# A decay factor's way to the partitions: one transfer of 128 pieces of 16 bytes, and a re-sorted instruction order, in a fused gated linear attention and MLP mixer

## The chip, the cores and the metric

The kernel runs on one core of a Trainium2 chip. The core has TensorE (PE in the profile; its weight loads are PEld), VectorE (DVE), ScalarE (ACT), GpSimd (POOL) and SyncE (SP), each with an instruction queue of its own, worked off in order. 16 DMA engines serve the transfers that SP and POOL issue here. The metric is the time of one execution on the device in microseconds (us). The kernel before takes 181.18 us in the median of three runs (180.58, 181.18 and 183.98).

## The reference

Inputs are q, k, v and f_logit of shape (4, 8, 768, 48): batch, heads, positions, head width. First comes a linear attention whose state decays by a gate per key channel, then an MLP mixer over tokens and channels.

```python
f = 1.0 / (1.0 + np.exp(-f_logit))
for t in range(S):
    state = f[:, :, t, :, None] * state + np.einsum('bhd,bhe->bhde', k[:, :, t], v[:, :, t])
    y[:, :, t] = np.einsum('bhd,bhde->bhe', q[:, :, t], state)
x = y.transpose(0, 2, 1, 3).reshape(B, S, H * D)          # (4, 768, 384)
h = np.maximum(x.transpose(0, 2, 1) @ w_tok1, 0.0) @ w_tok2   # 768 -> 256 -> 768
u = x + h.transpose(0, 2, 1)
out = u + np.maximum(u @ w_ch1, 0.0) @ w_ch2              # 384 -> 1536 -> 384
```

## The kernel before

The 768 positions of a batch are cut into six chunks of 128. Within a chunk the recurrence is turned into matrix products. With S(t) the running sum of -log f from the chunk's start, the queries are scaled by exp(-S), the keys by exp(S), and the state is carried from chunk to chunk with the factor exp(-S(127)), one number per head and key channel.

The steps of one chunk, with the names and lines that the change and the prediction touch:

- `gates` (L473, L474, L479): ACT makes exp(-f) and L = log(1 + exp(-f)); DVE or POOL makes `Llo`, the part of L that its upper 16 bits lose. L is read as two bf16 halves. In batch 2 the planner chooses DVE or POOL for Llo, in batch 3 it is POOL.
- sums (L535 to L547): PE multiplies by a triangle of ones and leaves the running sums in a PSUM bank. For the first two batches it makes, in the same bank, the sums of the whole chunk with the key channels on the partitions (eight products with a column of ones).
- `G`, `Gi` (L559, L557): ACT makes exp(-S) and exp(S), and DVE scales q and k (L579).
- transposes (L589), copies of them (`qkT`, L455, L602), scores (L496), the mask product (`AmT`, DVE, L626), the products of keys and values (L512).
- the factor of the chunk, `glast[4]`, tiles of 128 partitions by 4 floats: partition = 64 x (head modulo 2) + key channel, column = head pair. In the first two batches it is an exponential of the column sums (L562). In the last two, ACT makes the exponential of the last 32 rows of the running sums in the natural layout into `ends` (L566), whose row 127 is the wanted one, and SP spreads that row over the partitions by DMA (L570 to L573), one transfer for each head pair.
- the state update on DVE (`tsum` L638, `state` L635 and L640, which read `glast`), two copies of it to bf16 (`state_bd`, L453 on ACT, L457 on POOL), and the chunk's output (L657 with the old state, L664 within the chunk), copied out as `x_bf` and `x_nat` (L453, L455).

From batch 1 on two chunks go together. When a batch's six chunks are there, `mixer` runs: tok1 (L694, relu into `h1T`, L462, L464), tok2 (L710) with the sums `x_nat` and `u_bf` (L726), transposes `ut` (L745), the first channel product "C1" (L762, 24 groups of three matmuls of 384 columns, relu into `zT`) and the second "C2" (L781, with the last sum on DVE, L787, and a store by SP, L791). The mixer of one batch runs mixed with the attention of the next.

All instructions are first written into a list of operations (`Plan`), with what each needs and makes, a rank (a due time) and a listed cost. `order` goes through them like a list scheduler: for each engine's ready operations it takes the one that could start first, counting a listed `lag`, then by rank. `SHIFTS` gives hundreds of operations, by their number, a rank and a lag of their own; such a table is the outcome of a search over orders. The resulting order is the program order, queue by queue; nothing is decided at run time, and the semaphores are put in for that order. Filler matmuls (L828) are put where the planner sees PE wait in the first 25 us. The bulk loads stand in POOL's queue among its computing (L394, L401), in a fixed order with computing sorted between them.

The operation of the transfer carries a listed cost: `("fix", 1900, 7000 if b == 2 else 4500, 520)`, that is 1900 ns of SP's time, 7000 or 4500 ns until the factor is there, and 520 ns of the wire.

Of the kernel before, what the change touches and what calls it, by code (L numbers as in the profile page):

```python
# [10 lines left out]
FP32 = mybir.dt.float32  # L11
# [9 lines left out]
    (24,60,100), (34,-50,2100), (40,-50,3100), (41,-50,1700), (50,50,1600), (73,-30,800), (76,0,600),  # L21
    (79,30,300), (80,60,700), (82,60,500), (84,90,1400), (98,300,800), (101,300,3200), (103,300,2200),
    (109,-106,0), (115,0,400), (116,0,600), (123,0,800), (124,0,800), (125,0,1200), (126,0,1100), (129,30,700),
    (130,30,300), (134,30,900), (138,30,1500), (141,30,900), (142,30,1000), (144,30,900), (146,30,1600),
    (148,30,2900), (149,30,3400), (150,60,1800), (154,60,600), (156,60,1600), (157,60,800), (163,60,2100),
    (164,60,2400), (165,60,1600), (167,60,1800), (168,60,1700), (169,60,1200), (170,60,600), (172,90,800),
    (173,90,1900), (176,90,1100), (177,90,500), (178,90,2500), (181,90,1500), (182,90,2000), (185,90,1900),
    (188,90,2700), (191,90,2900), (193,90,3100), (196,120,1100), (198,120,1200), (199,120,1500),
    (200,120,1500), (201,120,1700), (202,120,2200), (204,120,700), (215,120,3700), (216,150,500),
    (217,150,1000), (219,150,1100), (220,150,700), (221,150,1400), (222,150,900), (223,150,2100),  # L30
    (224,150,2400), (225,150,1900), (227,150,2800), (229,150,2500), (230,270,1800), (231,270,2300),
    (238,191,2300), (239,275,3600), (244,275,1500), (246,280,1000), (251,281,600), (253,301,3100),
    (257,302,2700), (258,283,1600), (262,284,1700), (265,284,3000), (269,285,300), (270,290,1200),
    (271,290,1500), (272,291,1300), (274,292,1300), (276,293,1200), (278,294,1200), (279,294,2300),
    (280,295,1000), (281,295,1500), (282,-89,0), (283,300,2000), (284,623,0), (286,310,200), (287,310,300),
    (288,-160,0), (289,315,2400), (290,-161,0), (292,53,0), (293,325,2200), (294,252,0), (296,335,100),
    (297,335,100), (298,-125,0), (299,340,2000), (300,446,0), (302,302,0), (303,350,1200), (304,947,100),
    (306,462,0), (307,360,600), (309,365,500), (310,164,0), (311,370,1200), (312,-610,200), (313,375,600),
    (314,914,0), (316,586,0), (318,157,0), (319,390,800), (320,395,300), (321,395,200), (322,-236,0),
    (323,400,1800), (324,312,0), (325,405,900), (326,410,100), (327,410,500), (328,415,100), (330,547,0),  # L40
    (332,770,0), (333,420,800), (335,690,0), (338,460,600), (341,513,100), (342,527,400), (345,1125,0),
    (347,567,300), (350,580,400), (355,620,200), (357,854,400), (363,318,0), (367,438,500), (370,449,0),
    (371,595,0), (373,490,700), (384,383,0), (385,370,300), (391,429,0), (400,360,2200), (401,360,700),
    (406,360,1000), (408,360,1400), (411,360,1100), (415,360,1000), (416,360,1800), (419,440,2200),
    (422,581,0), (423,440,500), (428,440,1300), (430,440,500), (439,440,1800), (440,440,1100), (442,440,2200),
    (444,440,600), (445,440,700), (446,440,900), (447,440,800), (451,440,400), (452,440,800), (457,520,800),
    (459,520,400), (465,520,200), (477,520,100), (478,520,300), (479,520,100), (480,413,0), (483,520,100),
    (486,580,400), (487,720,400), (490,580,300), (492,581,400), (494,821,400), (504,563,0), (508,583,600),
    (516,580,100), (518,581,500), (520,582,500), (523,583,900), (525,584,900), (526,797,0), (527,585,900),
    (528,420,0), (531,697,600), (532,302,0), (534,645,0), (535,711,900), (536,809,0), (538,307,0), (542,837,0),  # L50
    (543,739,900), (544,860,0), (546,852,0), (548,829,0), (550,812,0), (552,427,0), (555,781,100), (556,873,0),
    (560,771,0), (561,802,500), (562,846,0), (564,670,0), (565,816,400), (566,915,0), (567,823,300),
    (568,1027,0), (570,652,0), (572,754,0), (573,844,1700), (574,745,0), (576,909,0), (578,1039,0),
    (579,860,300), (581,966,0), (587,965,200), (588,980,100), (591,995,100), (592,1010,600), (593,1025,300),
    (594,995,600), (596,1381,0), (597,855,0), (610,590,300), (616,690,300), (618,790,400), (621,790,400),
    (622,790,600), (623,790,1000), (625,620,100), (627,869,0), (630,620,500), (631,620,1100), (633,754,0),
    (634,815,0), (638,620,600), (639,620,1500), (645,620,1800), (646,620,1300), (648,620,2600), (651,620,200),
    (652,620,1600), (653,620,1600), (654,620,1500), (660,620,700), (661,720,400), (662,720,1100),
    (663,720,1200), (664,720,1000), (666,720,1400), (668,720,600), (669,363,500), (670,720,700), (671,720,200),
    (672,720,800), (677,880,0), (682,720,800), (684,720,1000), (689,720,1100), (690,789,0), (691,720,900),  # L60
    (693,720,800), (697,720,500), (698,720,100), (699,869,0), (701,820,1100), (705,920,0), (706,820,300),
    (720,820,700), (721,820,600), (723,906,0), (724,820,1600), (725,820,1600), (745,780,0), (748,823,0),
    (751,919,0), (753,972,1900), (756,973,1700), (757,969,0), (760,975,300), (761,975,600), (762,975,1400),
    (769,1130,0), (770,973,800), (777,1399,300), (778,1087,900), (785,1166,0), (786,1115,1200), (787,1072,0),
    (789,1269,0), (791,1206,0), (793,1193,0), (795,1043,0), (797,1109,0), (798,1157,900), (803,1178,300),
    (804,1178,1100), (805,1105,300), (806,1185,800), (807,1192,200), (809,1090,0), (811,1206,700),
    (812,1206,1900), (813,1213,400), (814,1213,2000), (815,1220,600), (816,1220,2200), (817,1227,800),
    (818,1227,1500), (821,1241,900), (822,1241,1700), (824,1265,300), (828,1295,3800), (830,1325,5400),
    (833,1340,1300), (834,1355,3200), (838,1385,1500), (840,1415,4500), (841,1385,5400), (845,1460,3700),
    (848,1475,1800), (849,1490,4600), (854,980,1200), (856,980,1600), (860,1080,3000), (863,1080,1900),  # L70
    (865,1180,1300), (870,1180,1400), (872,1010,2500), (885,1010,200), (891,1010,1000), (892,1010,400),
    (894,1010,700), (895,1010,700), (898,1010,1700), (899,1010,900), (900,1010,1600), (902,1010,800),
    (907,1010,1100), (908,1039,0), (911,1110,800), (913,959,1000), (915,1110,1900), (916,1099,0),
    (918,1110,800), (919,1110,600), (921,1110,600), (922,1175,0), (923,1110,800), (928,1110,700),
    (929,1110,1200), (933,1110,4200), (934,1438,0), (938,1110,1000), (939,1110,1200), (944,1110,2500),
    (945,1110,2200), (946,1210,300), (947,1210,1000), (948,1210,1200), (949,1210,800), (951,1210,800),
    (957,1210,1900), (970,1210,1300), (971,1210,2300), (973,1210,3200), (976,1210,2100), (977,1210,3200),
    (978,1360,1000), (985,1361,900), (992,1360,1400), (994,1360,5900), (995,1361,2200), (998,1362,3100),
    (1000,1362,4500), (1001,1363,2000), (1004,1364,2900), (1005,1364,3300), (1006,1364,8300), (1007,1365,3800),
    (1008,1365,5000), (1011,1360,5100), (1017,1363,6600), (1019,1364,4700), (1021,1365,7000), (1022,1470,3000),  # L80
    (1023,1470,7300), (1025,1477,4600), (1027,1484,3900), (1028,1491,5200), (1030,1498,3900), (1032,1505,5300),
    (1035,1512,3700), (1036,1519,5900), (1037,1519,5900), (1038,1526,5700), (1040,1533,4600), (1044,1547,5300),
    (1047,1554,6700), (1048,1561,4800), (1052,1575,5100), (1056,1423,0), (1060,1603,5600), (1062,1610,4900),
    (1063,1610,6000), (1065,1617,4600), (1066,1624,5900), (1068,1631,5800), (1075,1685,5400), (1085,1775,5700),
    (1090,1820,5600), (1092,1850,4700), (1095,1865,4800), (1096,1880,5100), (1102,1929,4900),
)
KEPT = 3
# [212 lines left out]
def kernel(  # L300
# [12 lines left out]
    nc = tc.nc  # L313
# [208 lines left out]
    def sums_and_turns(b, c, r):  # L522
# [42 lines left out]
        elif not last:  # L565
# [4 lines left out]
            def across():  # L570
                row = ends[i][127:128].rearrange("o (hp par) d -> o hp (par d)", par=2)
                for hp in range(HP):
                    nc.sync.dma_start(out=glast[g4][:, hp:hp + 1], in_=row[:, hp])  # L573
# [288 lines left out]
```

## Time and profile before

| what | value |
|---|---|
| median of three runs | 181.18 us |
| the profiled execution | 180.21 us |
| its span | 178.5 us |
| PE busy | 168.8 us (95%) |
| DVE, ACT, POOL busy | 130.7, 117.7, 84.9 us |
| clock granted to PE | 1.0 throughout |
| factor transfers (L573) | 40, of 0.5 KB each |
| packets of SP's and POOL's DMA queues | 15600 and 78960 |

The profile is taken of one execution; its own time lies 1.71 us above its span. An engine's busy time says how full it is, not what ends a stretch. On PE each matmul's record overlaps the next, so the distance between starts tells what one costs. In a list of waits, each line gives the waiting group, what ended its wait, the time in total, how often, and the longest.

### The profile page before, as it was taken

The page shows a single profiled execution, that of the slowest core. Times are in us where ns is not written, and L with a number is a line of the kernel's source. Part 1 is how long each engine was busy: PE and PEld are TensorE (multiplying, and loading weights), DVE is VectorE, ACT ScalarE, POOL GpSimd, SP SyncE. Part 2 cuts the span into 40 slices and gives each one's busy share as a digit, 9 for nine tenths or more (in the row PEclk, how much of TensorE's full clock was granted, in tenths as well). Part 3 has the DMA queues.
Part 4 walks back from the last instruction along what each step waited for, and adds up shares of the span by engine and source line. Part 5 has one row for each costly group of instructions (what it writes and reads, how often), then busy time and mean ns, then how long its engine had stood idle before and what let it go on. Part 6 is the DMA issues. An engine that isn't in the chain of part 4 may idle for free.

```text
span 178.5 us, 4470 instructions
## 1 busy us (share of the span) xinstructions
PE 168.8 (95%) x1739; PEld 108.0 (61%) x1739; DVE 130.7 (73%) x284; ACT 117.7 (66%) x272; POOL 84.9 (48%) x111
## 2 busy tenths in 40 slices
PE   6989977999999998999999999999999999999992
PEld 2446545566767765666667565766676666667660
DVE  6789876968987999995969777988967375423231
ACT  4589794869984398989899847488864333376000
POOL 7999968639299659589444750330111011000000
PEclk9999999999999999999999999999999999999999
DMA  7999999999999999999999990110001002210132
GB/s 106 122 163 160 142 207 217 242 147 194 165 141 174 220 167 189 52 109 91 231 131 118 190 141 19 45 47 1 6 2 44 4 2 93 82 48 0 44 132 88
DMA packets 94581, 19.97 MB, mean 112 GB/s; under 512 B 87296, under 2 KB 93744, under 8 KB 94560
## 3 DMA queue, kind: packets, MB, share of 16 engines
q0 software_dynamic: 78960, 13.77, 96.4%
q1 hardware_dynamic: 15600, 5.92, 13.8%
q8 instruction: 13, 0.21, 0.5%
q14 instruction: 8, 0.07, 0.1%
HBM read 25.17 MB, written 4.72 MB: 167 GB/s over the span
## 4 chain that ended last, share of the span: by engine, by line
PE 66%; DVE 9%; ACT 7%; issue 6%; DMA 4%; POOL 4%; SPq 1%; DVEq 0%; ACTq 0%; POOLq 0%
PE ps L781 20%; PE ps L762 20%; PE ps L589 4%; PE ps L710 4%; DMA f_sb<-in_f_logit_dram 3%; PE ps L496 2%; PE ps L828 2%; PE ps L694 2%; POOL qk_sb L394 2%; DVE AmT L626 2%; PE ps L745 2%; PE ps L664 2%; PE ps L512 1%; DMA glast<-ends 1%; PE ps L547 1%
## 5 line engine op out<-in xcount | busy, mean ns | idle before, releaser
L781 PE MATMUL ps<-w_ch,zT 128*128 128x384 bf16 (+2 forms) x300 | 52.7, 320 | 0.0
L762 PE MATMUL ps<-uT,w_ch 128*128 128x384 bf16 x288 | 51.3, 326 | 0.0
L462 ACT ACTIVATE zT<-ps 128x384 bf16<-128x384 f32 x71 | 34.2, 490 | 14.5 <-PE ps L762 12.1
L781 PEld LDWEIGHTS <-zT 128*128 128x128 bf16 x300 | 27.6, 98 | 16.5 <-issue 0.5
L762 PEld LDWEIGHTS <-w_ch 128*128 128x128 bf16 x288 | 27.0, 98 | 16.5
L626 DVE TENSOR_TENSOR AmT<-ps,tri_bf 128x512 bf16<-128x512 f32 x46 | 30.3, 683 | 5.5 <-PE ps L496 5.5
L787 DVE TENSOR_TENSOR x_nat<-x_nat,ps 128x384 f32<-128x384 f32 (+2 forms) x25 | 13.3, 533 | 14.1 <-PE ps L781 12.0
L394 POOL DMA_DIRECT2D qk_sb<-in_q_dram x19 | 18.5, 974 | 9.1 <-DMA w_ch<-in_moe_w_ch_dram 3.4
L394 POOL DMA_DIRECT2D qk_sb<-in_k_dram x19 | 18.9, 993 | 5.4 <-DMA f_sb<-in_f_logit_dram 4.3
L394 POOL DMA_DIRECT2D v_sb<-in_v_dram x19 | 18.7, 982 | 2.7 <-ACT L L474 2.4
L464 DVE TENSOR_SCALAR zT<-ps 128x384 bf16<-128x384 f32 x25 | 13.4, 554 | 7.2 <-PE ps L762 6.6
L579 DVE TENSOR_TENSOR qk<-qk_sb,GG 128x768 bf16<-128x768 bf16 (+1 forms) x30 | 14.3, 481 | 3.2 <-ACT GG L559 2.3
L589 PE MATMUL ps<-ident,qk 128*128 128x128 bf16 x192 | 15.0, 219 | 1.4 <-DVE qk L579 1.4
L457 POOL CAST state_bd<-state 48x192 bf16<-48x192 f32 x16 | 5.6, 352 | 21.8 <-DVE state L640 12.7
L589 PEld LDWEIGHTS <-qk 128*128 128x128 bf16 x192 | 11.9, 97 | 4.6 <-DVE qk L579 3.1
L828 PE MATMUL ps<-steady 128*128 128x512 bf16 x39 | 12.8, 438 | 1.5 <-DVE steady L426 1.5
L473 ACT ACTIVATE f_sb<-f_sb 128x384 f32<-128x384 f32 x24 | 11.9, 519 | 3.6 <-DMA f_sb<-in_f_logit_dram 3.4
L557 ACT ACTIVATE GG<-ps 128x384 bf16<-128x384 f32 x24 | 11.6, 488 | 1.8 <-PE ps L547 1.7
L726 DVE TENSOR_TENSOR x_nat<-x_nat,ps 128x384 f32<-128x384 f32 x21 | 10.9, 548 | 2.5 <-PE ps L710 2.5
L474 ACT ACTIVATE L<-f_sb 128x384 f32<-128x384 f32 x24 | 12.1, 522 | 0.3
L602 DVE COPY qkT<-ps 128x1024 bf16<-128x1024 bf16 x18 | 12.0, 683 | 0.4 <-PE ps L589 0.2
L559 ACT ACTIVATE GG<-ps 128x384 bf16<-128x384 f32 x24 | 11.6, 488 | 0.9 <-PE ps L547 0.5
(71 smaller groups left out, 244.2 us busy)
## 6 DMA issues: line engine op xcount, KB each, us to landing
out_dram<-x_nat SPq DMA_DIRECT2D x23, 192.0 KB, 1.9
f_sb<-in_f_logit_dram POOLq DMA_DIRECT2D x3, 1152.0 KB, 10.4
qk_sb<-in_k_dram POOLq DMA_DIRECT2D x18, 96.0 KB, 6.4
qk_sb<-in_q_dram POOLq DMA_DIRECT2D x18, 96.0 KB, 6.2
v_sb<-in_v_dram POOLq DMA_DIRECT2D x18, 96.0 KB, 6.4
f_sb<-in_f_logit_dram SPq DMA_DIRECT2D x6, 192.0 KB, 4.6
w_ch<-in_moe_w_ch_dram POOLq DMA_DIRECT2D x2, 576.0 KB, 10.2
w_ch<-in_moe_w_ch_dram POOLq DMA_DIRECT2D x1, 1152.0 KB, 14.6
```

The costliest lines, as they stand in the source:

```text
L394: lambda eng=eng, into=into, of=of: eng.dma_start(out=into, in_=of),
L462: nc.scalar.activation(out_, in_, AF.Relu, bias=0.0, scale=1.0)
L464: nc.vector.tensor_scalar(out_, in_, 0.0, None, ALU.max)
L474: add(ACT, r, lambda: nc.scalar.activation(full, fb, AF.Ln, bias=1.0, scale=1.0), need=[key], make=[whole], kind=el)
L579: add(DVE, r, lambda n=n: nc.vector.tensor_tensor(qk[i][:, n, :, 0:D], qk_sb[nb][:, n, :, c, :], GG[i][:, n], ALU.mult), need=[(x, nb, c) ...
L589: nc.tensor.transpose(to[:, o + hp, :], blk(src)[:, hp, :], ident)
L602: add(DVE, r, lambda: nc.vector.tensor_copy(qkT[i], banks[p_t[0].at].bitcast(BF16).rearrange("p (n t) -> p n t", t=C)), make=[("qkT", i, 0 ...
L626: add(DVE, r, lambda half=half, made=made: nc.vector.tensor_tensor(half, made(), tb4, ALU.mult), need=["tri_bf"], make=[("AmT", i, p)], ba ...
L762: nc.tensor.matmul(banks[pm.at][:, 0:384], lhsT=w[:, kt, c0:c0 + 128], rhs=uT[:, kt, cols], start=(kt == 0), stop=(kt == 2))
L781: nc.tensor.matmul(banks[pm.at][:, 0:n1 - n0], lhsT=zT[:, kt, tt * 128:(tt + 1) * 128], rhs=w_ch2[:, kt, n0:n1], start=(kt == 0), stop=(kt ...
L787: add(DVE, rank("ch2", tt), lambda un=un, pm=pm, n=n1 - n0: nc.vector.tensor_tensor(un, un, banks[pm.at][:, 0:n], ALU.add), make=[("x_nat" ...
L828: nc.tensor.matmul(banks[NBANK - 1], lhsT=steady[:, 0:128], rhs=steady, start=True, stop=True)
```

## The change

Four things change together:

1. `ends` is laid out as 128 x (2, 64, 4): parity of the head, channel, head pair, in place of 128 x (8 heads, 64 channels). The four factors of one partition lie side by side in 16 bytes.
2. The exponential that fills it writes through a permuted view: neighbouring channels lie 16 bytes apart.
3. One transfer of 128 pieces of 16 bytes takes the place of four transfers of 128 pieces of 4 bytes.
4. The listed cost of the operation becomes 600 ns, 5200 or 3400 ns, and 300 ns, and `SHIFTS` is another table. So the order of all queues differs. The operations themselves are the same, but for some that may go to either of two engines, and 38 filler matmuls for 39.

```diff
-    ends = [st([128, H, 64], FP32, f"ends{i}") for i in range(2)]
+    ends = [st([128, 2, 64, HP], FP32, f"ends{i}") for i in range(2)]
...
             add(ACT, r, lambda: nc.scalar.activation(
-                ends[i][96:128, :, 0:D], sview()[96:128], AF.Exp, bias=0.0, scale=-1.0),
+                ends[i][96:128, :, 0:D].rearrange("t par d hp -> t hp par d"),
+                sview()[96:128].rearrange("t (hp par) d -> t hp par d", par=2), AF.Exp, bias=0.0, scale=-1.0),
                 make=[("ends", i)], bank=p_s, kind=el)

             def across():
-                row = ends[i][127:128].rearrange("o (hp par) d -> o hp (par d)", par=2)
-                for hp in range(HP):
-                    nc.sync.dma_start(out=glast[g4][:, hp:hp + 1], in_=row[:, hp])
+                nc.sync.dma_start(out=glast[g4], in_=ends[i][127:128].rearrange("o par d hp -> o (par d) hp"))

             add(SP, r, across, need=[("ends", i)], make=[("glast", g4)],
-                kind=("fix", 1900, 7000 if b == 2 else 4500, 520))
+                kind=("fix", 600, 5200 if b == 2 else 3400, 300))
...
 SHIFTS = (
-    (24,60,100), (34,-50,2100), (40,-50,3100), (41,-50,1700), (50,50,1600), (73,-30,800), (76,0,600),
+    (6,-30,200), (24,60,1500), (26,60,1800), (40,-50,3400), (42,-50,2300), (44,-50,2000), (46,-50,3600),
...
```

In the changed order, as far as the prediction uses it: in batch 1 the state update of chunk 4 stands on DVE ahead of the last mask product of the pair; the sums of batch 2's chunk 1 come ahead of the last output of batch 1, so that ACT has G, Gi and `ends` of one chunk ahead of `h1T`; Llo of batch 2's chunk 2 is POOL's, behind ten loads, another Llo and the load of f for batch 3; then come the state copies of chunks 0 and 1 and the load of k; two Llo of batch 3 stand on POOL between the loads of q and v. The last stretch of PE is as before: C1 and then 84 matmuls of C2.

## Prediction

> **What bounds the kernel now.** I read four views in this order: the page's busy times, the waits of each engine, the chain of the last microseconds, and the order in time around the places where TensorE stood still.
>
> ```profile
> PE 168.8 (95%) x1739; PEld 108.0 (61%) x1739; DVE 130.7 (73%) x284; ACT 117.7 (66%) x272; POOL 84.9 (48%) x111
> PEclk9999999999999999999999999999999999999999
> ```
>
> PE is the bound, at full clock. Its busy time covers overlapping matmuls, so the chain says better how dense it is:
>
> ```profile
> 155.06 8.29 PE ps L762 x51
> 163.35 11.74 PE ps L781 x84
> ```
>
> 51 matmuls of 384 columns in 8.29 us are 162.5 ns each, and the last 20 us hold nothing else. So time can only come out of PE's standstills. The waits of PE, over the whole span:
>
> ```profile
> PE ps L589 <- DVE qk L579: 1.4, 3, 0.8
> PE ps L657 <- ACT state_bd L453: 1.1, 2, 0.6
> PE ps L710 <- DVE h1T L464: 0.5, 1, 0.5
> PE ps L710 <- ACT h1T L462: 0.4, 2, 0.3
> PE ps L745 <- DVE u_bf L726: 0.3, 1, 0.3
> PE ps L547 <- POOL Llo L479: 0.2, 1, 0.2
> ```
>
> The named waits count idle time alone. Between matmul starts the losses are larger by the pipeline's depth (0.54 idle at 69.19 is 0.70 between starts). Counted that way from 34 us on, where the first mixer begins, I find 0.70 at 69.2, 0.43 at 72.5, 0.38 at 99.3, 0.33 at 109.7, 0.31 at 140.1 and 0.27 at 57.0: 2.4 us in all. Ahead of 34 us some 5 us more are lost beside the 39 filler matmuls. None of these waits names a factor DMA, and neither does any wait of DVE, the engine that reads what it brings (L635, L640). Last, the line of the source that issues it:
>
> ```profile
> L573 SPq DMA_DIRECT2D glast<-ends x40: 469/594/1467, 70.2 to 131.5; - x40
> ...
> DMA to landing us min/median/max: 1.9/2.8/7.8
> ```
>
> The reader is to see the issue's cost on SP (ns, least, median, most) and the latency, long only where other transfers run.
>
> **The transfer itself.** Ten chunks (five in each of the last two batches) lose three of four issues: 30 issues of 0.594 us (median of L573), 17.8 us of SP's time. SP is idle most of the span, and behind these issues stand only stores of finished rows, for which nobody waits: worth 0. Latency: issues start 0.60 to 0.64 us apart, so the fourth lands about 3 x 0.6 + 2.0 = 3.8 to 3.9 us after the first issue where the queues are quiet (landing 1.9 to 2.1 after 108 us), and 6.0 to 8.7 us where the last batch's bulk loads run (82 to 107 us, landing up to 7.8). One transfer: 1.9 to 2.1 quiet, 4 to 7.8 loaded. No row shows 16-byte pieces. Bounds: not under 1.9, the least landing of the 4-byte ones; not over 2.9 quiet, what the 192 KB stores of that stretch take. I take 2.0, because the piece count of one transfer stays 128. Gain by itself: 0, since the factors lie ready 2.7 us and more before the state update that reads them. If that cover were gone (a chunk's sums put closer than 5 us of PE work to its use), lateness would cost its own length.
>
> **The exponential that feeds it (L566 before).** Ten of 0.483 us. It now writes floats 16 bytes apart. Rows of ACT with 384 elements lie between 0.47 and 0.52 whatever they write (L474, which writes 48 of each 64 floats, 0.522). No row has such a spacing, so bounds: 0 to a doubling, +0.48 each. I take 0, with the rows nearest to it, and keep 1.0 us for the range, because only two or so of the ten stand ahead of something PE waits for (the h1T at 71.97 stands behind two of them). The Trainium skill, page "SBUF — State Buffer", section "Door 1: The DMA port swizzle", speaks against this edit: accesses need two hits in a 16-byte line to run at full rate, and here each float is alone in its line. No run here shows it yet; by it the ten would be slower, by up to my upper end as an estimate.
>
> **The new order.** This is where the time can move: every queue is re-sorted. PE does the same matmuls but 38 fillers for 39 (-0.22, though a filler only stands in a wait). PE runs its list in order, so I laid both lists out and summed the issue intervals of what stands between a producer and its consumer: 0.49 for three 384-column matmuls, 0.45 for eight transposes, 0.55 for sixteen scores. What follows compares these covers with what the link needs.
>
> - Standstill at 69.2 (0.70): chunk 5 of batch 1 waits for the state copies of chunk 4. Cover after the value products is 3.46 us in both. DVE in order of time shows the update behind a mask product, which it does not need:
>
> ```profile
> 66.58 0.34 DVE L638 TENSOR_TENSOR tsum<-state,ps 128x192 f32<-128x192 f32 x1
> 66.84 0.68 DVE L626 TENSOR_TENSOR AmT<-ps,tri_bf 128x512 bf16<-128x512 f32 x1
> 67.44 0.92 DVE L640 TENSOR_TENSOR state<-tsum,glast 128x192 f32<-128x192 f32 x1
> ```
>
>   Now the update stands ahead of that product (0.60), so the copies can start 0.6 earlier; then the last mask product is late, behind an addition of 0.47, but it still ends before the old 69.1. Gain 0.5 to 0.7, taken 0.6.
> - 72.5 (0.43): the h1T of ACT stood behind three gate and two `ends` exponentials that wait on sums issued just before. Now one sum of batch 2 stands behind, and ACT has G, Gi, ends, then h1T; cover 0.98 in both, need about 0.75 (0.48 and the pipeline). Gain 0.4.
> - 99.3 (0.38): Llo of batch 3 stood behind the load of v on POOL, which waited for room. Now two Llo stand ahead of that load, and the first of these sums comes 3.2 us of PE work later. Gain 0.4.
> - 57.0 (0.27): cover from transposes to scores 1.30 for 1.18. Gain 0.1. 109.7 and 140.1: covers 1.10 for 0.98, and 0.97 for 0.97. Gain 0.
> - Head: the last x_bf on DVE no longer stands behind an x_nat copy (28.11, 0.47), so the last tok1 group is bound by ACT's x_bf (ends 28.86) and not by DVE's (29.13): 0.26. ACT's u_bf copies lose one x_nat between them (0.39), and the first C1 begins ahead of the last transposes. Together 0.5. Chunks 0 and 1 are read out later, with 3 to 4 us of cover: 0.
> - New tight places: transposes to scores of chunk 5 in batch 1, cover 0.49 and 0.28 of the other chunk's scores, need 0.95 (qkT copy 0.68): 0.2 lost. Chunks 0 and 1 there, 0.97 for two copies: 0.1. Reading out chunk 0 of batch 3, cover 1.77 for two mask products (1.36 and the pipeline), and chunk 3, 2.44 for mask, sum, update and two POOL copies: 0.2 together.
> - Llo of chunk 2 in batch 2 was on DVE and is now on POOL, behind eight loads (0.90 each), another Llo (0.83), two more loads and the 2.26 load of f. The Llo ahead of all these end near 67.5 (69.05 before, with one L fewer ahead of them on ACT): 67.5 + 7.2 + 0.8 + 1.8 + 2.3 + 0.8 = 80.4. Its L stands on ACT behind five relus, which can make it 82.4. PE comes to the sum after 69.8 us of listed work; before, the clock ran 11.1 ahead of the listed work at 69.2 and 11.8 at 82.2, so about 81.3. Loss 0 to 1.1; taken 0.4.
>
> Gains 0.6 + 0.4 + 0.4 + 0.1 + 0.5 = 2.0; losses 0.2 + 0.1 + 0.2 + 0.4 = 0.9. Net 1.1 from the profiled execution's 180.21 (span 178.5 and 1.71 around it): **179.1**. That execution is 0.97 under the median shown (181.18) and 0.37 under the fastest run (180.58), so a median of the changed kernel may lie up to 1 above what I name. About 2% is what a measurement of this kernel can tell from no change: 3.6 us, more than all standstills after 34 us together.
>
> **Rivals.** (1) The new order trades standstills one for one: 180.2, within 2%. For it: two covers are unchanged, and the order was laid out with listed costs, not with these rows. (2) Slower: POOL's line between 67 and 83 us. It carries Llo of chunk 2, then four state copies, then the 2.27 load of k. If a load there waits for room as one did before,
>
> ```profile
> 83.40 2.27 POOL L394 DMA_DIRECT2D qk_sb<-in_k_dram x1
> ...
> 91.53 2.22 POOL L394 DMA_DIRECT2D qk_sb<-in_q_dram x1 [3.40 <-issue]
> ```
>
> the Llo ends at 80.4 + 3.4 = 83.8 and PE stands 2.5 us at 81.3, in place of the 0.4 taken: 179.1 + 2.1 = 181.2. The state copies behind it (0.36 each, done at 84.5 for the first chunk) are read 1.3 us after that sum and add nothing. It decides against the change once that Llo ends after 82.8 (81.3 + 0.4 + the net 1.1); two such waits in the line make it 184.6, over 2%. Against it: what waited at 91.5 was a 576 KB load behind two large ones; those ahead of this Llo are 96 KB each but for f. (3) The strided exponential doubles: 0.48 ahead of four links, two covered: 179.1 + 1.0 = 180.1. The skill's line rule above is this rival's. (4) The transfer does not do what it says, pieces of 16 bytes costing as four did: 3.9 instead of 2.0. The tightest new link, chunk 2 of batch 3 (sum to its use 7.4 us of PE work, need 1.0 + 2.0 + 1.8), would still hold: 179.1.
>
> **Chances.** Forecast (177.8 to 179.9) 0.43, rival 1 0.2, rival 2 0.24 (half of it with a second wait or like misses elsewhere, beyond 2%), rival 3 0.1, rival 4 0.03. The range takes in rival 2 with its one wait (181.2), the median's offset (1.0) and half of rival 3 (0.5), and below it the losses of the new tight places at nothing and the head's gain at double (179.1 - 0.9 - 0.5): 177.6 to 182.7. Faster by over 2% needs 176.6, nearly all standstills gone: 0.05. Slower by over 2%: 0.12. Within: 0.83.
>
> **What would show it.** One issue per chunk landing in about 2.0 after 108 us; `ends` at 0.48; no wait of PE for state copies near 68, for h1T near 71, for Llo near 102; PE's last row still about 20 us of C1 and C2. Wrong: a wait of PE for Llo near 82, long gaps before POOL's loads there, `ends` near 0.8 or above, or a first C1 later than 34.2.

## The result, and the profile after

The changed kernel takes 182.08 us in the median of 13 runs (181.21 to 183.26), the kernel before 181.12 us in 13 runs beside them. The ratio is 1.0075 with a 95% interval of 1.0049 to 1.0101: slower by 1.4 us (0.0075 x 181.12), where the forecast was faster by 1.1. The profiled execution of after took 182.05 us, its span is 180.3. That is 1.84 over the profiled execution of before (180.21, 178.5). The two medians lie 0.96 us apart; the ratio, which comes with an interval, is what the text goes by. Ratios below are against the kernel before, each run beside its own runs of it. A few executions ran at a lower granted clock (one of e2 took 219.22 us at 0.755, and the profiled one of e3 285.77 us at 0.564), and the ratios are taken without such executions.

First the page of after, busy times and clock:

```profile
PE 169.5 (94%) x1734; PEld 108.5 (60%) x1738; DVE 131.0 (73%) x282; ACT 121.0 (67%) x275; POOL 84.5 (47%) x110
...
PEclk9999999999999999999999999999999999999998
```

PE and its clock are as before. ACT has 3.3 us more. Where they sit is seen in the lines of the exponential and of the transfer (least, median and most ns, then the first and last start), and under them the latency of the transfer:

```profile
L564 ACT ACTIVATE ends<-ps x10: 852/863/873, 69.0 to 127.2; 32x384 f32<-32x384 f32 x10
L570 SPq DMA_DIRECT2D glast<-ends x10: 469/475/560, 69.9 to 128.1; - x10
...
DMA to landing us min/median/max: 1.9/2.6/4.1
```

The transfer does what was forecast: one issue in place of four, landing in 1.93 to 1.95 where the queues are quiet (one 2.4), 2.7 to 4.1 beside bulk loads. The exponential does not: 0.863 us in place of 0.483, so 3.8 us for the ten. Next the waits of PE over the whole span (those of the filler matmuls, 1.5 and 0.2 us, are left out; the forecast's list leaves out its 1.5 too, and two waits of 0.2):

```profile
PE ps L586 <- DVE qk L576: 1.6, 4, 0.5
...
PE ps L543 <- DVE Llo L477: 0.7, 2, 0.4
PE ps L691 <- DVE x_bf L453: 0.6, 2, 0.4
PE ps L707 <- DVE h1T L462: 0.5, 1, 0.5
PE ps L494 <- DVE qkT L453: 0.4, 1, 0.4
PE ps L742 <- ACT u_bf L451: 0.2, 1, 0.2
```

The waits that the forecast took away are gone: none for the state copies (1.1 before), none for ACT's h1T, none for POOL's Llo. Others stand in their place after 34 us: for `x_bf`, for `qk`, for `u_bf`. The waits for DVE's `Llo` (0.7) and for `qkT` (0.4) lie ahead of 34 us. The end of the chain is still dense, 48 matmuls in 7.80 us and 84 in 11.74, followed by the last sum:

```profile
156.60 7.80 PE ps L759 x48
164.40 11.74 PE ps L778 x84
176.16 0.56 DVE x_nat L784
```

The last sum begins 1.04 us later than before (176.16 for 175.12). The span ends 1.8 later, so another 0.8 is lost behind the last matmul. The wait of SP's queue for that store in after:

```profile
SPq L854 <- DMA out_dram<-x_nat: 1.4, 1, 1.4
```

It names 1.4 us, but the store lands 1.82 us after its issue, as before (1.83). What follows the landing is in the records of SP's last instructions, taken from the trace of the two kernels (the time in us at which the wait is over, and the semaphore waited for, by number):

```text
before: 71 transfers of SP, the last on 117    after: 41 transfers, the last on 108
175.70  issue of the last store                176.75  issue of the last store
176.15  108                                    178.58  108 (store landed 178.57)
176.21  110                                    178.65  110
...                                            178.72  112
176.46  116                                    179.16  114
177.55  117 (store landed 177.53)              ...
177.61  118                                    179.44  118
177.67  drain                                  179.51  drain
178.49  end                                    180.34  end
```

SP's transfers take eight semaphores in turn, and at the end of the program SP waits for all eight in a fixed order. With 71 transfers the last store is on the next to last of them, and the six ahead of it are over while the store is under way. With 41 it is on the first, and the seven others follow the landing, with one step of 0.44 among them (what it waits for the trace does not name): 0.96 from landing to end before, 1.77 after, 0.8 us.

### The profile page after: what moved, and what is told of

Read it like the earlier page. It is cut to its first block, busy times and chain, and to the rows that moved or that the text cites. A ratio compares the mean times of both kernels' runs of the same rounds, so it can differ in the third digit from the quotient of the medians.

```text
span 180.3 us, 4391 instructions
## 1 busy us (share of the span) xinstructions
PE 169.5 (94%) x1734; PEld 108.5 (60%) x1738; DVE 131.0 (73%) x282; ACT 121.0 (67%) x275; POOL 84.5 (47%) x110
## 4 chain that ended last, share of the span: by engine, by line
PE 52%; DMA 17%; ACT 9%; POOL 9%; DVE 6%; issue 4%; POOLq 0%; DVEq 0%
PE ps L759 19%; PE ps L778 17%; DMA w_ch<-in_moe_w_ch_dram 8%; DMA f_sb<-in_f_logit_dram 6%; POOL qk_sb L392 5%; PE ps L586 3%; POOL v_sb L392 3%; DMA qk_sb<-in_k_dram 2%; PE ps L707 2%; PE ps L494 2%; PE ps L691 2%; DVE qk L576 2%; PE ps L742 2%; ACT ends L564 1%; ACT f_sb L471 1%
## 5 line engine op out<-in xcount | busy, mean ns | idle before, releaser
L759 PE MATMUL ps<-uT,w_ch 128*128 128x384 bf16 x288 | 52.6, 326 | 0.1
L460 ACT ACTIVATE zT<-ps 128x384 bf16<-128x384 f32 x74 | 35.6, 490 | 17.2 <-PE ps L759 12.2
L462 DVE TENSOR_SCALAR zT<-ps 128x384 bf16<-128x384 f32 x22 | 12.0, 554 | 9.0 <-PE ps L759 8.0
L576 DVE TENSOR_TENSOR qk<-qk_sb,GG 128x768 bf16<-128x768 bf16 (+1 forms) x30 | 16.1, 547 | 2.6 <-ACT GG L557 1.7
L825 PE MATMUL ps<-steady 128*128 128x512 bf16 x34 | 10.9, 430 | 1.8 <-DVE steady L424 1.5
```

What stands on the lines that cost most here:

```text
L460: nc.scalar.activation(out_, in_, AF.Relu, bias=0.0, scale=1.0)
L462: nc.vector.tensor_scalar(out_, in_, 0.0, None, ALU.max)
L576: add(DVE, r, lambda n=n: nc.vector.tensor_tensor(qk[i][:, n, :, 0:D], qk_sb[nb][:, n, :, c, :], GG[i][:, n], ALU.mult), need=[(x, nb, c) ...
L759: nc.tensor.matmul(banks[pm.at][:, 0:384], lhsT=w[:, kt, c0:c0 + 128], rhs=uT[:, kt, cols], start=(kt == 0), stop=(kt == 2))
```

## The experiments

Two explanations were set against each other at first. **Theory A**: the slower exponential, in front of what PE waits for, and the later end cost more than the new order brings. **Theory B**: the new order itself is worse. The edits are given against the kernel that each starts from.

### e1 to e4: the order, and the way the exponential writes

Old transfer in the new order (e1), and the new transfer in the old order (e2):

```diff
 e1, against after
-    ends = [st([128, 2, 64, HP], FP32, f"ends{i}") for i in range(2)]
+    ends = [st([128, H, 64], FP32, f"ends{i}") for i in range(2)]
-                ends[i][96:128, :, 0:D].rearrange("t par d hp -> t hp par d"),
-                sview()[96:128].rearrange("t (hp par) d -> t hp par d", par=2), AF.Exp, ...
+                ends[i][96:128, :, 0:D], sview()[96:128], AF.Exp, bias=0.0, scale=-1.0),
-                nc.sync.dma_start(out=glast[g4], in_=ends[i][127:128].rearrange(...))
+                row = ends[i][127:128].rearrange("o (hp par) d -> o hp (par d)", par=2)
+                for hp in range(HP):
+                    nc.sync.dma_start(out=glast[g4][:, hp:hp + 1], in_=row[:, hp])
 e2, against before: the same lines the other way round; SHIFTS and the listed cost stay those of before
```

In e3 (against after) and e4 (against e2) the exponential writes in memory order, and reads PSUM 384 bytes apart instead:

```diff
-                ends[i][96:128, :, 0:D].rearrange("t par d hp -> t hp par d"),
-                sview()[96:128].rearrange("t (hp par) d -> t hp par d", par=2), AF.Exp, ...
+                ends[i][96:128, :, 0:D],
+                sview()[96:128].rearrange("t (hp par) d -> t par d hp", par=2), AF.Exp, ...
```

Expected of e1:

> The changed kernel's order of all queues, but the row of factors written and moved as before (natural layout, four transfers of 4-byte pieces a chunk). Theory A: the changed kernel's extra 1.3 us has three parts: the exponential that writes 16 bytes apart (0.86 us in place of 0.48, on PE's path at some of the ten places, 0.6 to 0.9 together), the wait for the last store at the program's end (0.5 to 0.8, because one of SP's semaphores waited for early now belongs to the last store), and the new order itself (0 +- 0.4). Then this kernel lies at 0 to +0.4 us against the one before, ratio 1.000 to 1.002. Theory B: the new order alone makes the loss: +1.3, ratio 1.007. If the longer way of four transfers (3.9 us in place of 2.0) is needed by the new order, PE waits for state copies after 100 us and it is slower still, 1.01.

Expected of e2:

> The order of before with the new layout, the strided exponential and the single transfer. Theory A: the exponential at 0.86 and the late end both cost here too: +0.5 to +0.8 from the end, +0.3 to +0.6 on PE near 72 and 110 us where h1T stands behind it: ratio 1.004 to 1.008. Theory B: 1.000.

Expected of e3:

> The changed kernel with one thing altered: the exponential walks its output in the order of memory, so that it reads PSUM 384 bytes apart in place of writing SBUF 16 bytes apart. If only the writing side is slow, it takes 0.48 again and the kernel gains 0.6 to 0.9 against the changed one (ratio to before 1.002 to 1.005, the late end and the order left). If reading PSUM with a stride costs as much or more, the exponential is at 0.86 or above and the ratio 1.007 or more.

Expected of e4:

> The order of before, the single transfer, and the exponential that writes in the order of memory and reads PSUM with a stride. Theory A: if that exponential is at 0.48, only the late end is left of the losses: +0.5 to +0.8, ratio 1.003 to 1.0045. Theory B: 1.000, since the order is that of before. Either way the single transfer by itself brings nothing, since nobody waits for it in this order.

| run | order | transfers per chunk | `ends` us each | ratio, 95% interval |
|---|---|---|---|---|
| after | new | 1 | 0.863 | 1.0075 [1.0049, 1.0101] |
| e1 | new | 4 | 0.482 | 1.0020 [0.9999, 1.0041] |
| e3 | new | 1 | 0.482 | 1.0009 [0.9982, 1.0036] |
| e2 | old | 1 | 0.858 | 1.0153 [1.0108, 1.0197] |
| e4 | old | 1 | 0.482 | 1.0047 [1.0018, 1.0076] |

The write is the cause, not the read: 16 bytes apart into SBUF costs 0.38 us per exponential, 384 bytes apart out of PSUM costs nothing. In the old order it costs most, since there `h1T` stands behind two of them on ACT. The exponential and the first of PE's waits in e2:

```profile
L566 ACT ACTIVATE ends<-ps x10: 845/858/879, 69.8 to 130.5; 32x384 f32<-32x384 f32 x10
```

```profile
PE ps L709 <- ACT h1T L462: 1.6, 2, 1.1
```

Before, that wait was 0.4 in total and 0.3 at most. Theory B falls with e2: the old order with the whole new transfer is slower than the changed kernel. Theory A named the causes, but not all sizes: e1 came out in its range and e4 just above (1.0047 for up to 1.0045), while e2 lies well above it (1.0153 for up to 1.008) and e3 below (1.0009 for at least 1.002).

### e5, e6, e7: an even number of stores

These test the end of the program. Two stores of batch 0 become one, so that SP issues 40 transfers, not 41, and the last store falls on the semaphore that is waited for last. e5 starts from e3, e6 from e4, e7 from after.

```diff
+        first = []
...
-                add(SP, rank("ch2", tt), lambda un=un, to=to: nc.sync.dma_start(out=to, in_=un),
+                op = add(SP, rank("ch2", tt), lambda un=un, to=to: nc.sync.dma_start(out=to, in_=un),
...
+                if b == 0 and tt in (1, 2):
+                    op.fn = lambda both=rows[1:3], xn=xn: first.append(xn) if not first else nc.sync.dma_start(
+                        out=both.rearrange("t p n -> p t n"), in_=x_nat[xn][:, 1:3, :])
```

> The changed kernel with the exponential of the ends writing in memory order (as in e3), and with two stores of batch 0 (token tiles 1 and 2) put together into one transfer, so that SP issues 40 transfers in place of 41; everything else, the order included, is that of e3. Theory A (the end of the program is a row of waits in a fixed order over the eight semaphores that SP's transfers take in turn; the last store's semaphore is waited for first when there are 41 of them and last when there are 40): the span ends about 0.9 us after the last store lands, in place of 1.74, and the time falls by 0.8 from e3's, to about 180.2, a ratio of 0.996 against the kernel before. Theory B (the late end of e4 and of the changed kernel belongs to the transfers of the factors themselves or to the run): the end stays at 1.74 after the landing and the ratio at 1.001.

> e4 (old order, one transfer, exponential in memory order) with the same two stores of batch 0 put together, so 40 transfers of SP. Theory A: 0.8 less than e4, a ratio of 1.000 against the kernel before (0.9975 to 1.0025), since then nothing is left of the change but the one transfer, and that is worth nothing. Theory B: e4's 1.0047 again.

> The changed kernel with the two stores put together and nothing else. Theory A: 0.8 less than the changed kernel, a ratio of 1.003 in place of 1.0075, and the last store on the semaphore that is waited for last. Theory B: 1.0075.

Measured: e5 0.9967 [0.9947, 0.9987], e6 0.9977 [0.9947, 1.0006], e7 1.0036 [1.0014, 1.0057]. That is 0.0042, 0.0070 and 0.0039 less than e3, e4 and after: 0.8, 1.3 and 0.7 us, each known to some 0.7, where the trace had 0.8. In e7 the last store lands at 178.99 and the program ends at 179.90, 0.91 later. SP's wait for that store is now short, since the other waits come first (the wait on SP's queue, the same line in e5 and in e7):

```profile
SPq L858 <- DMA out_dram<-x_nat: 0.5, 1, 0.5
```

So the late end is shown, and e5 is faster than the changed kernel; against the kernel before, its interval lies just below 1, but that of its repetition (e14, 0.9979 [0.9946, 1.0011]) does not. The exponential can now be priced where nothing else differs: e7 less e5 is 0.0069, 1.25 us (plus or minus 0.5), in the new order; e2 less e4 is 0.0106, 1.9 us (plus or minus 1.0), in the old. Where it enters is seen near 120 us, in the order in time of ACT and DVE. After:

```profile
119.08 0.49 ACT L555 ACTIVATE GG<-ps 128x384 bf16<-128x384 f32 x1
...
119.59 0.86 ACT L564 ACTIVATE ends<-ps 32x384 f32<-32x384 f32 x1
...
120.47 0.49 ACT L557 ACTIVATE GG<-ps 128x384 bf16<-128x384 f32 x1
...
120.99 0.56 DVE L576 TENSOR_TENSOR qk<-qk_sb,GG 128x768 bf16<-128x768 bf16 x1 [0.43 <-ACT GG L557]
```

and e5:

```profile
118.60 0.49 ACT L555 ACTIVATE GG<-ps 128x384 bf16<-128x384 f32 x1
...
119.11 0.48 ACT L564 ACTIVATE ends<-ps 32x384 f32<-32x384 f32 x1
...
119.62 0.49 ACT L557 ACTIVATE GG<-ps 128x384 bf16<-128x384 f32 x1
...
120.14 0.56 DVE L576 TENSOR_TENSOR qk<-qk_sb,GG 128x768 bf16<-128x768 bf16 x1
```

From G's start to the start of `qk` it is 1.91 us in after and 1.54 in e5: DVE waits 0.43 for the second factor, and PE stands 0.46 at 121.61 ahead of the transposes, which is missing in e5. The same happens near 75: `ends` at 71.76 pushes two `u_bf`, and PE loses 0.65 at the transposes ut; e5 has nothing there. Near 106 two short gaps of PE (0.25 together) stand behind ACT's state copy and `x_bf`, which follow the `ends` of 104.64. e5 has neither gap. By the table of lost time further down, after loses 0.58 more than e5 between 71 and 87 us and 0.36 more from 108 us on; with the 0.25 that is 1.2, in line with the price.

### e8, e10, e11, e12: GpSimd's subtractions beside DVE

After has a standstill of 0.67 at 97.9 that no exponential explains. Its order in time there (start, length, how many, and in brackets the idle time ahead and what ended it):

```profile
94.54 2.40 POOL L477 TENSOR_TENSOR Llo<-L 128x384 bf16<-128x384 f32 x3
...
94.60 3.24 DVE L576 TENSOR_TENSOR qk<-qk_sb,GG 128x768 bf16<-128x768 bf16 x2
...
97.89 0.23 PE L586 MATMUL ps<-ident,qk 128*128 128x128 bf16 x1 [0.50 <-DVE qk L576]
```

Two products take 3.24 where others take 1.1. The record of the first alone runs from 94.60 to 97.37, across all three subtractions, which end at 96.94. In e8, these three subtractions take 48 elements per partition for 384, and the other heads' remainders are left out. e10 and e11 do so in batches 2 and 3 of after and of before (but for the last chunk of batch 2). In e12 the three are done on DVE, in e5.

```diff
 e8 (against after)
+        if b == 3 and c >= 3:
+            op.fn = lambda a=lo[:, 0:1], f=full[:, 0:1], h=hi[:, 0:1]: nc.gpsimd.tensor_tensor(a, f, h, ALU.subtract)
 e10 (against after), e11 (against before)
+        if b == 3 or b == 2 and c < SPLIT:
+            op.fn = lambda: nc.gpsimd.tensor_tensor(lo[:, 0:1], full[:, 0:1], hi[:, 0:1], ALU.subtract) if op.engine == POOL \
+                else nc.vector.tensor_tensor(lo, full, hi, ALU.subtract)
 e12 (against e5)
+        if b == 3 and c >= 3:
+            op.fn = lambda: nc.vector.tensor_tensor(lo, full, hi, ALU.subtract)
```

> The changed kernel with the remainder Llo of chunks 3, 4 and 5 of batch 3 (three subtractions on POOL near 94 to 97 us) taken for one head of eight only: 48 elements per partition in place of 384; the other heads' remainders are left as they were, so this part of the computation is left out. It asks what made the product qk of DVE near 94.6 us take some 2.7 us for one operation, after which TensorE stood 0.67 us at 97.9. Theory A (DVE was held by POOL's subtractions, which run back to back beside it): the two products there take about 0.55 each, as elsewhere, the standstill of 0.67 is gone, and the time is 0.3 to 0.7 under the changed kernel's, ratio 1.004 to 1.006. Theory B (DVE's long product is a wait of its own that the profile doesn't show): it stays near 2.7 us and so does the standstill.

> The changed kernel with every remainder Llo on POOL taken for one head of eight (batch 3 all, batch 2 chunks 0, 1, 3 and 4; the one of chunk 5 of batch 2 stays whole); the other heads' remainders are left out of the computation. Theory A (a DVE operation that reads two tiles of SBUF stands until POOL's subtraction has ended: in the changed kernel the state update at 65.34 took 0.83 where it takes 0.36, and 0.57 of standstill followed at 69.3; qk at 94.6, 0.67 at 97.9): both long operations fall to 0.36 and 0.55, the standstill at 69.3 to about 0.26 and the one at 97.9 to nothing; ratio 1.001 to 1.004 where the changed kernel had 1.0075 and e8 1.0047. Theory B (only the stretch near 94 hangs on it): 1.0047 again.

> The kernel before with the same remainders on POOL taken for one head of eight (batch 3 all, batch 2 chunks 0, 1, 3 and 4), the other heads' left out. It shows what the collision costs in the old order, where the state update at 67.44 took 0.92. Theory A (the new order loses more by it than the old): 0.997 to 1.000, so 0 to 0.5 us less than the kernel before, against 0.7 to 1.1 us less in the changed kernel. Theory B (both lose alike): the same difference in both.

> e5 with the three subtractions Llo of batch 3, chunks 3, 4 and 5 done on DVE in place of POOL, at the same place of the order; nothing is left out. DVE pays 3 x 0.55 for them and is rid of POOL beside it there, where the two products qk took 2.0 us in place of 1.1. Theory A (the collision is the cost): DVE's line is 0.7 us longer at 97, and it was late by 0.37 already, so the standstill near 97.7 stays or grows to about 1.0, ratio 0.997 to 1.000; no better version than e5. Theory B (DVE has room there): the standstill goes, ratio 0.994 to 0.996.

In e8 the products are back at 0.55 beside the short subtractions, and what DVE waits for is ACT:

```profile
95.61 1.13 POOL L479 TENSOR_TENSOR Llo<-L 128x48 bf16<-128x48 f32 x3
...
95.61 0.55 DVE L578 TENSOR_TENSOR qk<-qk_sb,GG 128x768 bf16<-128x768 bf16 x1
...
96.85 0.56 DVE L578 TENSOR_TENSOR qk<-qk_sb,GG 128x768 bf16<-128x768 bf16 x1 [0.69 <-ACT GG L559]
```

PE's standstill there is gone. In e10 the state update at 66.46 takes 0.36 (0.83 at 65.34 in after), and the standstill of 0.57 ahead of tok1 falls to 0.32. The one product that is still long in e10 (1.03 at 75.16) stands beside the one subtraction that was left whole. Nor is every DVE operation held: beside the subtractions of after, the mask products, which read PSUM and one tile of SBUF, take 0.68 and `tsum` 0.34, as they do elsewhere. So the mechanism is shown: a DVE operation that reads two tiles of SBUF can be held while POOL's subtraction reads SBUF. The Trainium skill, page "SBUF — State Buffer", section "Who interferes with whom", says that a DVE instruction with two SBUF inputs contends with a GpSimd instruction that reads SBUF, and that the later of the two is held until the other ends. These traces agree in the main: the product of 94.60 starts 0.06 behind a subtraction and takes 2.77 us for 0.55, while one that starts 0.17 ahead (74.41 in after) takes 0.55 and the subtraction 1.06 for 0.82. They also show one DVE operation held by three subtractions in a row. The starts in the records do not settle every case: in e9 a product that starts 0.29 ahead of the subtractions takes 2.33.

What it is worth in time is less clear than the profile made it. e8 has 1.0047 [1.0030, 1.0064] and e10 1.0055 [1.0030, 1.0080] where after has 1.0075: 0.4 to 0.5 us, which these intervals do not tell from nothing; e10's expectation of up to 1.004 was missed. e11, the old order, has 0.9965 [0.9938, 0.9992], 0.6 us, though its median is all but that of the kernel before (181.13 and 181.20). So theory A of e11, that the new order suffers more, is not borne out. The collision hangs on where the two engines happen to meet in an execution. The lines of the products in e5 and in e14 (below) are those of one and the same program:

```profile
L576 DVE TENSOR_TENSOR qk<-qk_sb,GG 128x768 bf16<-128x768 bf16 x18 | 10.8, 602 | 2.2 <-ACT GG L557 2.0
```

```profile
L576 DVE TENSOR_TENSOR qk<-qk_sb,GG 128x768 bf16<-128x768 bf16 x18 | 9.9, 552 | 1.8 <-ACT GG L557 1.7
```

The first has 0.9 us of held products, the second none. In the second, on another chip, the first product near 95 starts 0.29 ahead, and it is the subtractions that take longer (0.94, 1.18 and 0.93 for 0.82), for which PE does not wait. e12 stands at 0.9959 [0.9928, 0.9990], and PE has no standstill near 97.7 in it (0.37 in e5). Its expectation A, that DVE would be late by the three subtractions, was wrong. It is not to be told from e5 (0.9967); its interval, too, lies just below 1.

### e9: cover for the scores of chunks 4 and 5

In after PE loses 0.74 us between 62 and 64 us, at the scores that follow the transposes of chunks 4 and 5 of batch 1. e9 puts 0.65 us of C2 ahead of them, in e5:

```diff
-    for op in plan.best(idle, 6500.0, 25500.0):
+    done = list(plan.best(idle, 6500.0, 25500.0))
+    late, scores = plan.ops[350], plan.ops[466]
+    done.remove(late)
+    done.insert(done.index(scores), late)
+    for op in done:
         op.fn()
```

> e5 with one group of TensorE work moved and nothing else: the four products of token tile 4 of batch 0 (C2, first third, some 0.65 us) are issued directly ahead of the scores of chunks 4 and 5 of batch 1 in place of nine groups earlier. In the changed kernel TensorE lost 0.7 us between 62 and 64 us, where the scores follow the transposes with 0.95 us of copy on DVE to wait for and a group of C1 whose read-out on ACT runs until 63.2. Theory A (the stretch is short of other work at that place, so 0.65 us more of it is worth nearly its length): 0.4 to 0.6 us of the loss goes, ratio 0.993 to 0.9945 where e5 had 0.9967. Theory B (DVE and ACT are the bound there; work moved from ahead of the transposes is missed where it was, since the products qk that feed the transposes come no earlier): the loss moves to the transposes or to the states, 0.1 us or less is gained, ratio 0.996 to 0.998.

Measured 0.9992 [0.9959, 1.0025], above the ranges of both theories. PE's order in time in e9:

```profile
59.57 0.81 PE L779 MATMUL ps<-w_ch,zT 128*128 128x384 bf16 x4
61.13 0.33 PE L654 MATMUL ps<-state_bd,qkT 128*128 128x96 bf16 x4 [0.75 <-ACT state_bd L451]
```

The scores no longer stand, but the state products ahead of them now wait 0.75 for ACT's state copy. Theory B is right on where the loss goes: PE waits there for the chain over DVE and ACT, and the work moved only moved the gap. The ratio does not price it, since e9's profile also has two held products near 96 (2.33 and 1.18 us).

### e13, e14: the transfer alone

e1 (four transfers, 1.0020) and e5 (one, 0.9967) left open whether the transfer itself is worth up to 1 us in the new order. e13 gives e5's tile and exponential four transfers, with the two stores apart (71 transfers, the last on the next to last semaphore). e14 is e5 again beside it.

```diff
-                nc.sync.dma_start(out=glast[g4], in_=ends[i][127:128].rearrange("o par d hp -> o (par d) hp"))
+                row = ends[i][127:128].rearrange("o par d hp -> o (par d) hp")
+                for hp in range(HP):
+                    nc.sync.dma_start(out=glast[g4][:, hp:hp + 1], in_=row[:, :, hp:hp + 1])
```

> e5 with its one transfer taken back: four transfers of 128 pieces of 4 bytes again, out of the same tile, written in memory order by the same exponential, in the same new order, and the two stores of batch 0 apart again, so that SP issues 71 transfers and the last store falls on the semaphore that is waited for next to last. It differs from e5 in the number of transfers alone. Theory A (the transfer is worth nothing, as forecast; e1's 1.002 against e5's 0.9967 came from where GpSimd's subtractions happened to fall beside DVE): within 0.4 us of e5 in the same comparison, ratio 0.996 to 0.999. Theory B (30 more transfers on the queues cost something in this order, though nobody waits for them by name: GpSimd's and SyncE's transfers share the engines, and what comes later moves the collisions): 0.9 us over e5, ratio 1.000 to 1.004.

> e5 again, on the same chip and against the same runs of the kernel before as e13: 0.9967 as before, if the difference to e13 is to be read at half a microsecond. Theory A of e13: e13 and this agree within 0.4 us. Theory B: this one is 0.9 us faster.

Measured: e13 0.9991 [0.9960, 1.0022], e14 0.9979 [0.9946, 1.0011], 0.2 us apart by the ratios and 0.6 by the medians (180.75 and 180.12). The transfer is worth nothing that these runs can tell: they exclude more than about 1 us. That e1 stood 0.96 us over e5 and e13 only 0.2 over e14 is within the scatter of such comparisons, and a few tenths for the transfer, by the interval up to 1 us, stay open.

## Why the prediction was wrong

The sum said -1.1 us, all of it from the new order. Measured is +1.4. From the runs: the exponential +1.25 (e7 less e5), the end +0.7 (after less e7), and all the rest, order and transfer, -0.6 (e5; -0.4 by e14). The three add up by the way they are formed, and each is known to some 0.5 us. The first two were not in the sum. The median, 182.08, lies in the stated range of 177.6 to 182.7, but by luck: the range reached that far for rival 2's wait, which did not come. (Its lower end, 179.1 - 0.9 - 0.5, is 177.7.) The forecast also took 2% as what can be told from no change; the interval here is 0.26% to either side.

**The step "I take 0" for the exponential failed.** The value was chosen by rows that write consecutive floats; the only thing that spoke of the spacing was a rule of the Trainium skill (page "SBUF — State Buffer", section "Door 1: The DMA port swizzle": full rate needs two hits in a 16-byte line). The measurement bears that rule out, at 0.863 for 0.482 us. The mechanism and the size of rival 3 were right (0.38 of up to 0.48 each, 1.25 us where 1.0 was named); what was wrong was its chance, 0.1, though no row spoke against it. A rival whose condition is a property of the edit itself, with no row like it, should not have been put at one in ten.

**A term was missing: the end of the program.** "Behind these issues stand only stores ... worth 0" counted SP's time, not its semaphores. Taking 30 transfers away moved the last store from the next to last place of the closing waits to the first: +0.8 us. The order of the closing waits was in the trace of before and could have been read there.

**The order's gains were there one by one, but not their sum.** To see this stretch by stretch, take for each matmul its start less the listed time of all PE work ahead of it; what this lag grows by in a stretch is what PE lost there. In us, with the stretches named by the times of before:

| stretch | before | forecast | after | e5 | e14 |
|---|---|---|---|---|---|
| to 42, the head | 9.86 | 9.4 | 9.30 | 10.40 | 9.79 |
| 42 to 71 | 1.33 | 0.9 | 2.09 | 1.67 | 1.81 |
| 71 to 87 | 0.58 | 0.6 | 0.78 | 0.20 | 0.20 |
| 87 to 108 | 0.62 | 0.4 | 1.20 | 0.62 | 0.24 |
| 108 on | 0.99 | 1.0 | 1.27 | 0.91 | 0.92 |
| sum | 13.38 | 12.3 | 14.64 | 13.80 | 12.96 |

Between the two profiled executions the lag's +1.26, the end's +0.8 and one filler less (-0.22) make up the 1.84.

- Head: forecast -0.5, and -0.56 in the profile of after. But ten profiles of the new order lie between 9.3 and 10.6 with a mean of 9.9, five of the old between 9.7 and 10.9 with a mean of 10.0. The gain was one execution's luck; on the average there is none.
- 42 to 71: forecast -0.4, measured +0.3 to +0.8 in the three profiles of the table. The wait for the state copies at 69.2 did go. DVE's order in time in after shows the update where the forecast had it, straight behind `tsum`:

```profile
64.97 0.34 DVE L635 TENSOR_TENSOR tsum<-state,ps 128x192 f32<-128x192 f32 x1
65.34 0.83 DVE L637 TENSOR_TENSOR state<-tsum,glast 128x192 f32<-128x192 f32 x1
```

  Its 0.6 was given back at the new tight place, the scores of chunk 5, priced at 0.2: 0.74 (0.73 in e5). There the price took the copy of DVE alone; e9 showed PE waiting for DVE and ACT in turn there. A further 0.26 to 0.57 stands ahead of tok1, where the last `x_bf` of DVE is late.
- 71 to 87: the 0.4 at `h1T` came (0.58 to 0.20 in e5), and the 0.4 put down for POOL's Llo near 81 did not; in after `ends` took the gain back.
- 87 to 108: the 0.4 for Llo of batch 3 came (0.62 to 0.24 in e14), and the 0.2 for the read-outs did not. In its place is the collision of POOL and DVE at 94 to 97, from nothing in e14 to 0.67 in after, which no step had. That a two-tile operation of DVE could be held was in the rows of before, the `state` of 0.92 quoted in the forecast (0.35 elsewhere). By this count the stretch loses 0.7 less in e8 and in e10 than in after; elsewhere they lost more, in the head above all.

**Rival 2, POOL's line, did not come.** POOL's order in time in after:

```profile
80.58 0.82 POOL L477 TENSOR_TENSOR Llo<-L 128x384 bf16<-128x384 f32 x1 [0.95 <-ACT L L472]
...
87.38 2.26 POOL L392 DMA_DIRECT2D qk_sb<-in_q_dram  x1 [0.98 <-issue]
```

The subtraction ended at 81.4, within 0.1 of the time at which PE was expected to need it, and waited for ACT and not for a load; no wait of PE is left there. The 3.4 us of idle time ahead of the load at 91.5, which the forecast read as a wait for room (the trace says `issue`), shrank to 0.98 and 0.97 ahead of two loads.

**Rival 1 was the nearest on the order itself.** With one transfer, exponential in memory order and the even number of stores in both, the new order (e5 0.9967, e14 0.9979) and the old (e6 0.9977) differ by 0.1 us, plus or minus 0.6. With four transfers the new order stands at 1.0020 (e1) and 0.9991 (e13). The gains and losses of the new order cancel as far as these runs can tell.

**Right were** the transfer (one issue, 1.9 to 4.1 us, waited for by nobody, worth nothing that e13 and e14 can tell) and the statement that the dense last 20 us stay.

## What to carry to other kernels

A layout that helps a transfer is paid by the engine that writes it: ask first whether the writing or the reading side can take the stride (here PSUM could, for nothing), and price a spacing that no row shows at its upper end. When transfers are added or removed, count them again to the last store, because the closing waits go by turn. And price a re-sorted order by several executions: single standstills of half a microsecond come and go between executions of the same program.

## What the runs showed of the hardware

- ACT writes 32 x 384 fp32 in 0.48 us when neighbours are 4 bytes apart and in 0.86 when they are 16 bytes apart in SBUF; reading PSUM 384 bytes apart leaves it at 0.48 (e3, e4).
- A transfer of 128 pieces within SBUF lands after 1.9 to 2.1 us on quiet queues with pieces of 4 bytes (before) and after 1.9 with pieces of 16 (after; one took 2.4).
- The closing waits of SP take 0.06 to 0.09 us each, with one step of 0.44 to 0.46 among them in after, e5 and e7, and those that stand behind the last landing lengthen the program: 0.96, 1.77 and 0.91 us from landing to end in before, after and e7.
- One DVE product of two SBUF tiles, 0.55 us alone, took 2.77 beside three subtractions of GpSimd in a row (after), and 0.55 beside short ones (e8). A DVE operation with one input from PSUM took the same beside them as alone (mask product 0.68, `tsum` 0.34).
